# A new order for the last 900 of 1215 hand-ordered pieces of an attention and feed-forward kernel

## The chip, the cores and the metric

The kernel runs on one core of a Trainium2 chip. The time is device microseconds (us) of one execution; a kernel is run several times and its median is what counts. TensorE (PE in the profile) multiplies matrices and writes to the eight PSUM banks, P in the profile; ScalarE (ACT) and VectorE (DVE) read those banks, apply functions and write to on-chip memory; GpSimd (POOL) and SyncE (SP) mainly start DMA transfers. Each of these engines works through its own queue in order.

## The reference

Four batches, eight heads, 768 tokens, head size 64. Three of the heads (0, 2 and 6) use plain causal attention, the other five see only the first four tokens and a window of 64. The result, 3072 tokens by 512, goes through two matrix products with a leaky rectifier between them.

```python
scores = np.matmul(q, k.transpose(0, 1, 3, 2)) / np.sqrt(64)
keep = causal & (is_sink | in_window)      # heads 1, 3, 4, 5, 7
keep = causal                              # heads 0, 2, 6
a = softmax(np.where(keep, scores, -1e9))
x = np.matmul(a, v)                        # to 3072 x 512
h = x @ w_in                               # 512 x 2048
g = np.maximum(h, 0) + alpha * np.minimum(h, 0)
out = g @ w_out                            # 2048 x 512
```

## The kernel before, in words

**Units.** Heads are taken two at a time, four pairs for each batch, so there are 16 units of attention, numbered 0 to 15. A unit's first head has number 0 within it, the second number 1. The two heads of a unit lie in the upper and the lower 64 of the 128 partitions of the query tile `qT` and the key tile `kT`. Unit numbers that leave 0 when divided by four hold two causal heads, those that leave 2 one causal and one windowed head, the others two windowed heads.

**Pieces.** The work is cut into 1215 named pieces, and the list `ORDER` gives the order in which they are issued. Each engine's queue is this list with the other engines' work left out: there is no scheduler that moves anything. The names mean, for unit `n`, head `h` and part `m`:

- `Lq`, `Lk`, `Lv`: loads from memory, issued from SP; `C..`: casts of what was loaded; `Dq`, `Dk`: transposes by DMA, issued from SP, of the cast queries and keys; `T..`, `t..`: the same by TensorE for the early units.
- `Sn.h.m`: one part of the scores of a head, into one PSUM bank. `sn.h.m`: ScalarE's exponential of it (L512 for causal heads, L560 and L562 for windowed ones), which empties the bank. `mn.h.m`: VectorE's masking. `An.h`: probabilities times values (L595). `an.h`: VectorE's normalisation (L605, L606), which empties that bank. `Xn`: transpose into the token tile `xT`, by DMA for units 4 to 14.
- `Pt.f`: first feed-forward product for token block `t` (L640); `pt.f` and `gt.f`: rectifier on ScalarE (L645) and VectorE (L652). `O0.s.u` and `o0.s`: second product for block 0 (L660) and its copy out (L666). `Qt.u.y`, `Zt.u.y`, `Dy.h`, `b1` to `b8`: second product for blocks 1 to 7 in seven partial products (L718), with the sums before and after them.

**Banks.** A piece that needs a PSUM bank takes, when it is recorded, the one that was given back longest ago (`take`, `give`). In the chip it then waits for the engine that empties that bank.

**Score sets.** From unit 4 on, `S` pieces are not issued at their own place. They are gathered, and issued together at the first piece that may not pass them (`beside_burst`, `emit_burst`). A gathered set is issued in one of two ways. If both halves hold at least 576 columns, or the set has a unit from 8 on with two heads of one kind, L473 issues it with 64-row matmuls, alternating between the two heads, so that each head uses its own half of the array. Here this is called a *paired* set. Otherwise L466 issues it one matmul after the other on all 128 rows, the other head's rows being zero: an *unpaired* set.

```python
        halves = [[x for x in burst if x[1] == hh] for hh in range(2)]
        columns = [sum(x[5].shape[1] for x in half) for half in halves]
        if min(columns) < SPLIT and not any(merged(x[0]) for x in burst):
            for x in burst:
                nc.tensor.matmul(*x[3:6], start=True, stop=True)
        else:
            at = [0, 0]
            while halves[0] or halves[1]:
                hh = min((h for h in range(2) if halves[h]), key=lambda h: at[h])
                to, keys, queries = halves[hh].pop(0)[3:6]
                own = slice(D * hh, D * hh + D)
                nc.tensor.matmul(to, keys[own], queries[own], start=True, stop=True)
```

A part of a causal head has 448 columns (units 4, 8, 12) or 488 (units 6, 10, 14), a part of a windowed head 352 and the third one 448.

Of the kernel before, what the change touches and what calls it, by code (L numbers as in the profile page):

```python
# [26 lines left out]
g1.0 P0.5.1 Tk5 P0.4.0 p1.8 P0.6 tk5.0 g1.8 p0.7 P0.4.1 g1.12 P0.5.2 P0.4.2 p0.6 tk5.1 P0.10 g0.7 p0.4 p0.10 g0.6
S4.0.3 s4.0.3 S4.0.0 P1.4 g0.4 Tk6 g0.10 S4.0.1 S5.1.0 m4.0.3 P1.6 p0.5 tk6.1 Ck7.0 near1 D1.0 P0.12 tk6.0 O0.0.0 g0.5
O0.0.1 p1.6 Lv7 p0.12 g1.6 p1.4 S6.1.1 D1.1 s5.1.0 s4.0.0 S5.1.1 S4.1.2 g1.4 m4.1.0 s4.0.1 s4.1.2 Z1.0.1 s6.1.1 s5.1.1
O0.1.0 S5.0.0 S4.0.4 S4.1.4 S4.1.1 g0.12 O0.1.1 s5.0.0 m4.0.5 s4.1.4 m4.0.0 Ck7.1 s4.1.1 ns S5.1.2 S4.0.2 S4.1.3  # L30
S5.0.1 O0.0.2 s5.1.2 s4.1.3 D2.1 O0.0.3 O0.2.0 s5.0.1 m6.1.1 S6.0.4 s4.0.4 S5.0.2 S6.1.0 D4.1 m5.0.0 s4.0.2 Z1.0.3
S6.0.0 m5.1.2 o0.0 S6.1.2 S4.1.5 Lq9 Cq7 Cv4 s5.0.2 m5.1.1 O0.1.2 D2.0 Tk7 s4.1.5 O0.2.1 Cv5 Tq7 m4.0.1 m5.0.2 s6.1.0
m8.1.2 s6.1.2 O0.1.3 tk7.0 m5.1.0 m4.0.4 tk7.1 A4.0 Ck8 s6.0.0 tq7 A5.1 m4.1.2 S6.0.5 o0.1 m4.1.1 O0.2.2 Cq8 Dk8.0
s6.0.5 O0.3.0 S7.1.1 S6.0.1 a4.0 a5.1 S6.0.3 s6.0.4 S7.1.0 m6.1.0 m4.1.4 S7.0.2 S7.1.2 m5.0.1 s6.0.3 O0.2.3 m6.1.2 Ck9
A5.0 s7.1.2 O0.3.1 Cv6 m4.1.5 S6.0.2 Cv7 m4.1.3 s7.1.1 Dq8 s6.0.1 O0.3.2 m6.0.4 o0.2 a5.0 m6.0.5 S7.0.0 s7.1.0 Dk9.0
s7.0.2 A6.1 O0.3.3 m6.0.1 S7.0.1 Cq9 m7.1.0 s6.0.2 m6.0.0 s7.0.0 A4.1 m7.0.0 S8.0.0 S8.1.0 s7.0.1 S8.0.5 m6.0.3 S8.1.3
m7.1.1 S8.0.3 a6.1 S8.1.1 m7.1.2 o0.3 s8.0.3 A6.0 X5 a4.1 s8.0.5 A7.1 Q1.0.1 m7.0.2 s8.1.3 s8.1.0 m7.0.1 m6.0.2 s8.1.1
A7.0 a7.1 b1.1.0 Dq9 S9.1.1 a6.0 a7.0 S8.0.2 Lq10 S8.1.4 S8.0.1 X4 Q1.0.2 S9.1.0 S9.0.1 s8.0.0 Z1.0.2 D3.1 S9.0.2
# [958 lines left out]
```

## Time and profile before

| | |
|---|---|
| Times of three runs | 222.39, 222.77, 223.88 us; median 222.77 us |
| Profiled execution | span 220.4 us from first to last instruction; what lies around the span is not in the trace, and the median is 2.4 us above it |
| Granted TensorE clock | 1.000 over the whole span |
| Busy | PE 214.5 us (97%), DVE 188.0 (85%), ACT 145.8 (66%), POOL 45.6 (21%) |
| DMA | 35.98 MB, mean 163 GB/s |

A busy PE is one that has a matmul in flight; the end of a matmul is modelled, and matmuls overlap, so the mean duration of one is longer than the distance from one to the next. Where matmuls follow each other, the distance is what the next one costs. The chain in the profile follows the last instruction back to what released it, and so tells which engine sets the end.

### The profile page before, as it was taken

The numbers are of one execution on the slowest core, as the hardware profiler recorded it, in microseconds if no ns is written. First come the engines' busy times: TensorE is split into PE (matmuls) and PEld (weight loads), VectorE is DVE, ScalarE is ACT, GpSimd is POOL, SyncE is SP. The second block draws the span as 40 slices with busy tenths as digits, with TensorE's granted clock in tenths as the row PEclk, the third lists the DMA queues.
The fourth block names the chain that finished last, engine by engine and source line by source line (L and its number), as shares of the span: only waits on it lengthen the run. The fifth ranks groups of instructions, "written<-read, shape, count | busy, mean of one in ns | idle before, by whom it ended". The sixth has DMA issues, their size and how long they took to land.

```text
span 220.4 us, 5779 instructions
## 1 busy us (share of the span) xinstructions
PE 214.5 (97%) x2210; PEld 158.0 (72%) x2210; DVE 188.0 (85%) x471; ACT 145.8 (66%) x314; POOL 45.6 (21%) x92
## 2 busy tenths in 40 slices
PE   8989999999999999999999999999999999999993
PEld 7879866765465865577899666757889645888882
DVE  6879849979989897999998998999999767997841
ACT  4789659989999795657953165799783066816230
POOL 6679980620031200000004110100000200001000
PEclk9999999999999999999999999999999999999999
DMA  6999999999999999979999998791004310002124
GB/s 187 319 233 222 307 241 231 227 201 218 205 245 167 259 162 222 198 182 193 211 215 174 228 184 194 176 187 42 4 1 123 103 79 0 0 3 95 51 93 147
DMA packets 89655, 35.98 MB, mean 163 GB/s; under 512 B 76676, under 2 KB 87964, under 8 KB 89628
## 3 DMA queue, kind: packets, MB, share of 16 engines
q1 hardware_dynamic: 83484, 26.35, 59.4%
q0 software_dynamic: 5824, 8.93, 17.8%
q8 instruction: 17, 0.28, 0.5%
q10 hardware_dynamic: 320, 0.34, 0.5%
q14 instruction: 10, 0.08, 0.1%
HBM read 27.58 MB, written 6.29 MB: 154 GB/s over the span
## 4 chain that ended last, share of the span: by engine, by line
PE 92%; DVE 3%; ACT 2%; issue 1%
PE P L640 36%; PE P L718 28%; PE P L595 7%; PE P L660 7%; PE P L473 4%; PE P L814 3%; PE P L456 2%; PE P L406 2%; PE P L466 1%; PE P L620 1%; DVE kT L435 1%; PE P L544 1%; DVE g L652 1%; ACT neg L645 1%; ACT kT L435 0%
## 5 line engine op out<-in xcount | busy, mean ns | idle before, releaser
L640 PE MATMUL P<-xT,w_in_b 128*128 128x512 bf16 (+1 forms) x512 | 89.6, 326 | 0.0
L652 DVE SCALAR_TENSOR_TENSOR g<-neg,oma,P 128x256 bf16<-128x256 f32 (+1 forms) x128 | 71.7, 607 | 11.4 <-ACT neg L645 11.0
L645 ACT ACTIVATE neg<-P 128x512 f32<-128x512 f32 x96 | 55.4, 602 | 30.3 <-PE P L640 15.7
L640 PEld LDWEIGHTS <-w_in_b 128*128 128x128 bf16 x512 | 49.2, 98 | 29.1 <-issue 0.3
L718 PEld LDWEIGHTS <-g 128*128 128x128 bf16 x480 | 45.7, 98 | 8.1 <-issue 0.8
L512 ACT ACTIVATE eR<-P 128x448 bf16<-128x448 f32 (+4 forms) x63 | 37.0, 627 | 4.8 <-PE P L505 2.2
L718 PE MATMUL P<-w_out_b,g 128*128 128x256 bf16 x320 | 39.0, 273 | 0.0
L736 POOL DMA_DIRECT2D out_dram<-ot x14 | 7.6, 545 | 115.6 <-ACT ot L760 37.9
L560 ACT ACTIVATE eS<-P 128x352 bf16<-128x352 f32 x45 | 20.8, 494 | 2.3 <-PE P L473 1.4
L606 DVE TENSOR_TENSOR xn<-P,rcp 128x448 bf16<-128x448 f32 (+1 forms) x32 | 19.4, 607 | 1.1
L571 DVE TENSOR_TENSOR eS<-eS,ms_near 128x352 bf16<-128x352 bf16 x45 | 15.8, 363 | 0.7 <-ACT eS L560 0.6
L660 PE MATMUL P<-w_out_b,g 128*128 128x512 bf16 x64 | 15.8, 379 | 0.2 <-ACT kT L429 0.2
L703 DVE TENSOR_TENSOR g<-g 128x1024 bf16<-128x1024 bf16 x20 | 13.7, 683 | 0.1
L456 PE MATMUL P<-qT,kT 128*128 128x192 bf16 (+14 forms) x68 | 11.1, 251 | 0.2 <-ACT eS L566 0.2
L595 PEld LDWEIGHTS <-eS 128*128 128x128 bf16 x260 | 10.0, 97 | 1.3
L595 PE MATMUL P<-vb,eS 128*128 128x65 bf16 x260 | 10.8, 193 | 0.0
L522 DVE TENSOR_TENSOR eR<-eR,mr_near 128x128 bf16<-128x128 bf16 (+5 forms) x54 | 10.6, 223 | 0.0
L473 PE MATMUL P<-qT,kT 64*128 64x176 bf16 (+10 forms) x164 | 10.4, 249 | 0.0
L718 PE MATMUL P<-w,g 128*128 128x256 bf16 x80 | 10.4, 273 | 0.0
L660 PEld LDWEIGHTS <-g 128*128 128x128 bf16 x64 | 5.6, 97 | 6.3 <-issue 1.1
L595 PE MATMUL P<-vb,eR 128*128 128x65 bf16 x276 | 10.0, 193 | 0.0
L595 PEld LDWEIGHTS <-eR 128*128 128x128 bf16 x276 | 9.4, 97 | 0.6 <-issue 0.2
(130 smaller groups left out, 267.8 us busy)
## 6 DMA issues: line engine op xcount, KB each, us to landing
out_dram<-ot POOLq DMA_DIRECT2D x18, 256.0 KB, 3.2
rows<-in_k_dram SPq DMA_DIRECT2D x21, 192.0 KB
rows<-in_q_dram SPq DMA_DIRECT2D x18, 192.0 KB
rows<-in_v_dram SPq DMA_DIRECT2D x17, 192.0 KB
rows<-in_v_dram SPq DMA_DIRECT2D x14, 196.0 KB
rows<-in_q_dram SPq DMA_DIRECT2D x7, 384.0 KB
w_out_b<-in_moe_w_out_dram POOLq DMA_DIRECT2D x4, 512.0 KB, 15.1
rows<-in_k_dram SPq DMA_DIRECT2D x9, 196.0 KB
```

Of the source, the lines that this page charges most:

```text
L456: nc.tensor.matmul(to, keys, queries, start=True, stop=stop)
L473: nc.tensor.matmul(to, keys[own], queries[own], start=True, stop=True)
L512: nc.scalar.activation(ebuf[n, hh][:, lo:hi].rearrange("p (x c) -> p x c", x=len(parts)), P[:, got[0]:got[0] + len(parts), 0:(hi - lo) // ...
L560: nc.scalar.activation(slots, sc[:, 0:352].rearrange("p (s c) -> p s c", c=176), AF.Exp, scale=scale)
L571: nc.vector.tensor_tensor(slots, slots, ms_near[:, 0:2, :] if m == 0 else ms_near[:, 1:3, :], op=ALU.mult)
L595: nc.tensor.matmul(pav[:, i, :], e[:, o:o + 128], vv[:, j, hh, 0:D + 1], start=(m == 0), stop=(m == len(terms) - 1))
L606: nc.vector.tensor_tensor(xn[n][:, 0:nt, D * hh:D * hh + D], pav[:, :, 0:D], rcp.to_broadcast([128, nt, D]), op=ALU.mult)
L640: nc.tensor.matmul(psg[:, w * i:w * (i + 1)], w_in_b[:, c, 128 * fb:128 * (fb + 1)], xT[:, c, o:o + w], start=(x == 0), stop=(x == 3))
L645: nc.scalar.activation(neg[t, f], bank(held["P", t, f][0]), AF.Relu, scale=-1.0)
L652: nc.vector.scalar_tensor_tensor(g_buf[t % 2][:, fb, 0:w], neg[t, f][:, c], oma[:, fb:fb + 1], bank(got[0])[:, c], op0=ALU.mult, op1=ALU.add)
L660: nc.tensor.matmul(bank(held["O", t, s][0]), g_buf[t % 2][:, f, 128 * s:128 * (s + 1)], w_out_b[:, f, :], start=(f == 0), stop=(f == 15))
L718: nc.tensor.matmul(q_bank(t, u, CHAIN[y]), left[t, u][y][:, f, :], right[y][:, f, :], start=(first and f == 0), stop=(f == 7), skip_group_ ...
```

## The change

Only the list `ORDER` changes. It holds the same 1215 names. Of the first 303, three (`m4.0.2`, `m8.0.2` and `m12.1.2`) go to later places; these three issue no instruction, since no mask ends in that part, so the first 300 of the new list do what the first 303 of the old one did. All others come in another order. SP's queue, with its loads, transposes and stores, has the same 152 instructions in the same order, and so has GpSimd's. TensorE has 2210 matmuls before and after, VectorE 471 instructions, ScalarE 316 with its three DMA issues.

What the new list does to the score sets follows from the functions above. The columns are those of the first and the second head. The first five sets (4.0.5; 4.1.0; 4.0.3; 4.0.0; 4.0.1 with 5.1.0) are the same in both, and unpaired; they have 2592 columns in 11 matmuls.

| Before: pieces in a set | columns | | After: pieces in a set | columns | |
|---|---|---|---|---|---|
| 6.1.1 5.1.1 4.1.2 | 0, 1152 | unpaired | 4.1.5 | 0, 448 | unpaired |
| 5.0.0 4.0.4 4.1.4 4.1.1 | 800, 896 | paired | 6.1.2 | 0, 448 | unpaired |
| 5.1.2 4.0.2 4.1.3 5.0.1 | 800, 896 | paired | 5.1.1 4.0.4 4.1.1 5.0.2 6.1.0 5.0.1 | 1248, 1152 | paired |
| 6.0.4 5.0.2 6.1.0 6.0.0 6.1.2 4.1.5 | 1424, 1248 | paired | 4.0.2 6.1.1 5.0.0 5.1.2 | 800, 800 | paired |
| 6.0.5 | 488, 0 | unpaired | 4.1.3 6.0.5 6.0.0 4.1.4 6.0.3 4.1.2 | 1464, 1344 | paired |
| 7.1.1 6.0.1 6.0.3 7.1.0 7.0.2 7.1.2 | 1424, 1152 | paired | 6.0.4 | 488, 0 | unpaired |
| 6.0.2 | 488, 0 | unpaired | 6.0.1 7.1.1 7.0.1 7.0.2 7.1.0 7.1.2 | 1288, 1152 | paired |
| 7.0.0 | 352, 0 | unpaired | 7.0.0 | 352, 0 | unpaired |
| 7.0.1 | 352, 0 | unpaired | 6.0.2 | 488, 0 | unpaired |
| 8.0.0 8.1.0 8.0.5 8.1.3 8.0.3 8.1.1 | 1344, 1344 | paired | 8.0.3 8.1.1 8.0.4 8.0.0 8.0.5 8.1.4 | 1792, 896 | paired |
| 9.1.1 8.0.2 8.1.4 8.0.1 | 896, 800 | paired | 9.1.1 9.0.2 9.1.2 9.0.1 9.0.0 8.1.5 | 1152, 1248 | paired |
| 9.1.0 9.0.1 9.0.2 8.1.2 | 800, 800 | paired | 8.0.2 9.1.0 8.0.1 8.1.3 | 896, 800 | paired |
| 8.1.5 8.0.4 9.0.0 9.1.2 | 800, 896 | paired | 10.1.1 8.1.0 10.0.1 10.0.3 | 976, 800 | paired |
| 10.1.0 | 0, 352 | unpaired | 11.1.1 10.1.0 10.1.2 10.0.2 10.0.5 11.0.1 8.1.2 10.0.4 | 1816, 1600 | paired |
| 10.0.1 10.0.4 | 976, 0 | unpaired | 10.0.0 | 488, 0 | unpaired |
| 10.0.0 | 488, 0 | unpaired | 11.0.0 11.1.0 11.0.2 11.1.2 | 800, 800 | paired |
| 10.0.3 | 488, 0 | unpaired | 13.0.2 12.0.0 12.1.5 12.1.0 | 896, 896 | paired |
| 10.0.5 10.1.2 11.0.1 11.1.1 10.1.1 11.0.2 | 1288, 1152 | paired | 13.0.0 12.0.3 12.1.4 13.1.0 | 800, 800 | paired |
| 10.0.2 11.0.0 11.1.2 11.1.0 | 840, 800 | paired | 12.1.3 12.0.4 12.0.5 13.1.2 | 896, 896 | paired |
| 12.0.0 12.1.2 | 448, 448 | paired | 12.1.1 12.0.1 12.1.2 12.0.2 | 896, 896 | paired |
| 12.1.4 12.0.2 12.0.5 13.1.0 | 896, 800 | paired | 14.1.2 13.0.1 14.0.5 13.1.1 | 840, 800 | paired |
| 12.0.1 13.1.2 12.1.5 13.0.0 | 800, 896 | paired | 14.0.2 | 488, 0 | unpaired |
| 12.1.0 12.1.3 13.0.1 12.0.3 | 800, 896 | paired | 14.0.4 | 488, 0 | unpaired |
| 12.0.4 12.1.1 14.1.2 13.1.1 14.0.3 13.0.2 | 1384, 1248 | paired | 14.1.1 14.0.3 14.0.1 15.1.1 14.0.0 15.1.2 | 1464, 1152 | paired |
| 14.0.2 | 488, 0 | unpaired | 14.1.0 15.0.1 15.0.0 15.1.0 15.0.2 | 1152, 704 | paired |
| 14.0.4 | 488, 0 | unpaired | | | |
| 14.0.1 | 488, 0 | unpaired | | | |
| 15.1.2 14.1.1 14.0.5 15.0.0 14.0.0 15.1.1 | 1328, 1152 | paired | | | |
| 15.0.2 15.1.0 15.0.1 14.1.0 | 800, 704 | paired | | | |

The diff, cut to the stretches that the prediction speaks of:

```diff
 ORDER = """
 ...
-S4.0.3 s4.0.3 S4.0.0 P1.4 g0.4 Tk6 g0.10 S4.0.1 S5.1.0 m4.0.3 P1.6 p0.5 tk6.1 Ck7.0 near1 D1.0 P0.12 tk6.0 O0.0.0 g0.5
-O0.0.1 p1.6 Lv7 p0.12 g1.6 p1.4 S6.1.1 D1.1 s5.1.0 s4.0.0 S5.1.1 S4.1.2 g1.4 m4.1.0 s4.0.1 s4.1.2 Z1.0.1 s6.1.1 s5.1.1
 ...
-b8.3.0 g4.14 P5.8 s12.0.0 S12.1.4 p5.12 s12.1.2 S12.0.2 b6.3.0 S12.0.5 S13.1.0 Lk15 P5.6 Dq14 s12.0.5 p5.8 g5.12 p5.6
 ...
+S4.0.3 s4.0.3 S4.0.0 P1.4 g0.4 Tk6 g0.10 S4.0.1 S5.1.0 m4.0.3 P1.6 p0.5 tk6.1 Ck7.0 near1 D1.0 P0.12 tk6.0 O0.0.0 p1.6
 ...
+Cq9 s6.0.1 s7.0.1 O0.3.2 S7.0.0 A4.1 s7.1.0 s7.0.2 m6.0.5 m7.0.2 s7.0.0 a4.1 S6.0.2 s7.1.2 Q1.0.1 S8.0.3 s6.0.2 s7.1.1
+m7.1.0 m6.0.4 m6.0.0 m6.0.3 S8.1.1 S8.0.4 S8.0.0 S8.0.5 m7.1.1 S8.1.4 b1.1.0 m6.0.1 X5 s8.0.4 s8.0.0 Z1.0.2 O0.3.3
+m7.1.2 Dq9 m7.0.1 o0.3 s8.0.5 m7.0.0 kfz2 A6.0 A7.1 Lq10 A7.0 a6.0 Q1.0.2 s8.1.1 a7.1 s8.1.4 S9.1.1 S9.0.2 s8.0.3 S9.1.2
+a7.0 S9.0.1 S9.0.0 S8.1.5 X4 s9.1.1 X6 s9.1.2 Q1.0.6 s9.0.2 D3.0 X7 Q1.0.5 s9.0.0 b2.1.0 S8.0.2 S9.1.0 m8.0.4 s9.0.1
 ...
+s8.1.2 m10.0.1 Z2.0.3 m10.1.1 s10.0.2 s11.1.1 s11.0.1 Lk12 Q2.1.5 s10.0.5 b4.2.1 Cv10 P3.2 s10.0.4 Cv11 Z2.0.2 Q2.1.6
 ...
+b6.3.0 Cq14 P4.0.0 g5.12 P4.0.1 p5.8 p4.7 g4.7 P5.10 s13.0.2 s12.1.0 g5.8 s12.1.5 S13.0.0 p4.0 S12.0.3 p5.10 m12.1.5
+S12.1.4 g4.0 S13.1.0 s13.0.0 m13.0.2 g5.10 s12.0.3 P5.4 m8.1.2 Q4.0.1 p5.4 s12.0.0 Q4.1.1 Dq14 Z4.0.1 s13.1.0 b1.4.0
+s12.1.4 S12.1.3 S12.0.4 S12.0.5 S13.1.2 s13.1.2 Q4.0.2 Dk14.1 g5.4 P5.14 m4.1.2 b1.4.1 Z4.0.3 s12.0.4 s12.1.3 S12.1.1
 ...
```

120 lines of the change are left out of this document (57 added, 63 removed).

## The prediction, made before the changed kernel had run

> **What bounds the kernel now.** I read the page's first lines, then the busy times by stretch, then TensorE's waits, then the chain.
>
> ```profile
> span 220.4 us, 5779 instructions
> ...
> PE 214.5 (97%) x2210; PEld 158.0 (72%) x2210; DVE 188.0 (85%) x471; ACT 145.8 (66%) x314; POOL 45.6 (21%) x92
> ...
> PE 92%; DVE 3%; ACT 2%; issue 1%
> ```
>
> The third line is the chain by engine: TensorE sets the end for 92% of the span. By stretches (columns: stretch, its length, busy us of PE, its weight loads, DVE, ACT, POOL, then granted clock, DMA share, GB/s):
>
> ```profile
> 20.00:55.00 35.00, 34.80 (x354) 24.14 (x352) 27.79 (x67) 29.52 (x57) 16.75 (x35) 1.00 1.19 237
> 55.00:114.00 59.00, 59.00 (x622) 39.66 (x622) 55.89 (x153) 45.77 (x113) 6.17 (x10) 1.00 1.10 206
> 114.00:140.00 26.00, 26.00 (x241) 18.85 (x239) 24.16 (x54) 11.47 (x24) 3.71 (x7) 1.00 0.97 193
> 140.00:165.00 25.00, 25.00 (x272) 19.01 (x271) 24.69 (x70) 22.07 (x54) 1.63 (x3) 1.00 0.40 75
> 165.00:218.00 53.00, 51.75 (x477) 40.15 (x475) 40.15 (x88) 22.34 (x52) 2.68 (x5) 1.00 0.21 69
> ```
>
> From 55 us on, where the new order begins to differ (O0.0.0 stands just before it), PE is never idle up to its last matmul; in the last stretch the 1.25 us missing are the end. A busy PE could still be a slow one, so two more views: all that PE waited for between 20 and 218 us, and two long pieces of the chain (start, length, what).
>
> ```profile
> PE P L660 <- ACT kT L429: 0.2, 1, 0.2
> ```
>
> ```profile
> 173.79 12.95 PE P L640 x60
> 200.93 15.84 PE P L718 x144
> ```
>
> One wait of 0.2 us, in the part that stays. 60 matmuls of 512 columns in 12.95 us are 0.216 us each, 144 of 256 columns in 15.84 us 0.110 each: (0.216 - 0.110) / 256 = 0.414 ns a column and 4 ns a matmul, the same rate in both places. So the time behind 55 us is PE's work, laid end to end. A new order can change it in two ways only: by the work in the score sets, and by waits where there are none now.
>
> **The change: score sets.** All other matmuls stay as they are. The price of a paired set comes from a large and a small one, of 1344 columns a head and of 448; each is followed by another line's matmul, so the distance of the starts is its cost.
>
> ```profile
> 73.12 0.75 PE L473 MATMUL P<-qT,kT 64*128 64x448 bf16 x11
> 73.80 0.38 PE L595 MATMUL P<-vb,eR 128*128 128x65 bf16 x7
> ```
>
> ```profile
> 140.12 0.36 PE L473 MATMUL P<-qT,kT 64*128 64x448 bf16 x2
> 140.42 0.50 PE L718 MATMUL P<-w,g 128*128 128x256 bf16 x3
> ```
>
> 0.68 and 0.30 us: (0.68 - 0.30) / (1344 - 448) = 0.424 ns for a column of the longer head, and 0.11 us fixed. The 2688 columns of the large set cost 0.25 ns each, against 0.414 one after the other: the two heads do run side by side, and the longer one sets the time.
>
> Now the table of sets is added up. Unpaired columns: before 9192 in 40 matmuls, after 6280 in 30. Paired, by the longer head of each set: before 17,352, after 19,272. Paired sets: 17 before and 17 after, so the fixed cost stays. In all 26,544 columns become 25,552: 992 fewer. At 0.414 ns that is 0.41 us, and ten unpaired matmuls at 4 ns are 0.04. **The sum of the work: -0.45 us.** It is small because the new sets are fuller but not better balanced: the shorter heads leave 1704 columns empty before and 2632 after (the set from 8.0.3 alone 1792 against 896).
>
> The Trainium skill, page "TensorE: Matmul & The Clock Gate", section "Back-to-back issue gap", gives for streams of loads and matmuls a sustained 81 ns at 128 columns and 131 ns at 512. By that slope, 0.13 ns a column, the 992 columns would be an estimated 0.13 us; the trace has 0.216 us for 512 columns, so the trace's rate stands.
>
> **The change: waits.** Here nothing can be gained, since PE waits for nothing now; only lost. What is new is how many banks a set takes at once: at most six before, once eight after. I looked where PE, if it ran without a stop, would reach work whose bank is still to be emptied. The rows: unpaired parts and other PE work from the chain, durations of groups, and ScalarE's pace in a run without idle time.
>
> ```profile
> 69.91 0.21 PE P L466 x2
> 70.12 0.87 PE P L660 x4
> 70.99 0.15 PE P L466 x2
> ...
> 72.55 0.64 PE P L595 x21
> ...
> 75.18 0.87 PE P L718 x8
> ```
>
> ```profile
> L640 PE MATMUL P<-xT,w_in_b 128*128 128x512 bf16 x256 | 60.0, 379 | 0.0
> ...
> L560 ACT ACTIVATE eS<-P 128x352 bf16<-128x352 f32 x45 | 20.8, 494 | 2.3 <-PE P L473 1.4 <-PE P L466 0.9
> ...
> L606 DVE TENSOR_TENSOR xn<-P,rcp 128x448 bf16<-128x448 f32 x24 | 15.0, 624 | 0.8
> ...
> L605 DVE RECIPROCAL rcp<-P 128x7 f32<-128x7 f32 x24 | 4.8, 198 | 1.8 <-PE P L595 1.7
> ```
>
> ```profile
> 68.00 0.46 ACT L560 ACTIVATE eS<-P 128x352 bf16<-128x352 f32 x1
> 68.34 0.26 ACT L562 ACTIVATE eS<-P 128x96 bf16<-128x96 f32 x1
> 68.47 0.48 ACT L560 ACTIVATE eS<-P 128x352 bf16<-128x352 f32 x1
> 68.82 0.61 ACT L512 ACTIVATE eR<-P 128x488 bf16<-128x488 f32 x1
> 69.27 0.63 ACT L666 COPY ot<-P 128x512 f32<-128x512 f32 x1
> ```
>
> ScalarE's starts lie 0.35 us apart behind a part of 352 columns, 0.13 behind 96, 0.45 behind 488. A matmul's result is there 0.16 us after the next one begins (379 ns against 216).
>
> *Place one, the set from 8.0.3.* ScalarE must first finish the set from 6.0.1: s6.0.1, six windowed parts with two short ends, s6.0.2, the last being s7.1.1, whose bank the new set needs. From that older set's first matmul: 0.2 + 0.16 until 6.0.1's scores are there, then 2 x 0.45 + 6 x 0.35 + 2 x 0.13 = 3.26, and 0.11 for the last one's tail: 3.7 us. PE by then has done the set (0.11 + 1288 x 0.424 = 0.66), 7.0.0 and 6.0.2 (0.15, 0.21), O0.3.2 (0.87), A4.1 (0.64) and Q1.0.1 (0.87): 3.40, and gets 0.2 further before it comes to that bank. It waits about 0.1 us; nothing at all if ScalarE runs a little closer than these rows, 0.6 if it comes late to s6.0.1, behind the copy o0.2 (0.47 from row to row behind 69.27).
>
> *Place two, Q1.0.6.* It takes a7.0's bank. VectorE does a6.0, a7.1 and a7.0 in a row, 3 x (0.198 + 0.624) = 2.47, plus 0.16; PE meanwhile A7.1 and A7.0 (13 matmuls each at 0.64 / 21: 0.79), Q1.0.2 (0.87) and the set from 9.1.1 (0.11 + 1248 x 0.424 = 0.64): 2.30. A wait of 0 to 0.4.
>
> *Place three, the eight-bank set.* Q2.1.5 right behind it needs the bank of s10.1.0, whose scores are second in their half: 704 x 0.424 + 0.16 + 0.494 = 0.95 us, against 0.11 + 1816 x 0.424 = 0.88 for the set. A wait of 0 to 0.2.
>
> Their ends together are 0 and 1.2 us. A start that PE finds late makes the next wait shorter, since the emptying engine has gained on it, so I take **+0.2 us**. No wait is charged elsewhere: VectorE and ScalarE do the same work, and the tail behind Q6.1.4 is issued in nearly the old order.
>
> Sum: -0.45 + 0.2 = -0.25 us, against the span 220.4, so 220.15; what lies around the span, 2.4 us to the median of 222.77, stays. **222.5 us.**
>
> **The rivals.**
>
> *Banks emptied too late.* Fuller sets hand ScalarE more parts at once, and places of the three kinds come again in the sets from 12.1.1 and 14.1.1. For it: the sums at the three places, which come out within a few tenths of zero. Against more than a few tenths at each: ScalarE is busy for 45.77 of 59 us and 22.07 of 25, so it can be late in bursts, but not on the whole. Price: all three ends, 1.2 us, less 0.45: 223.5. It decides from 0.45 us of waits on: beyond that the change is **slower than before**. The Trainium skill, "TensorEngine Tiling (Array Packing)", section "PSUM Bottleneck", states this rule: tiling speeds up TensorE but not the emptying of PSUM. Before, the trace does not show it: PE waits for none of its 17 paired sets.
>
> *VectorE becomes the bound.* It has 24.69 of 25 us at 140 to 165 and 55.89 of 59 before. For it: each idle stretch that the new order opens there cannot be made good, as 0.31 us are all that is left. Against it: total work is the same, and Cv14 leaves the full stretch for an earlier one. Two to four us lost would give 224.3 to 226.3.
>
> *The transposes come late.* SP issues in order; Dq14 now waits for Cq14, which has moved behind the first P4.0 piece, and Dk14.1, Dk14.0 and Dq15 queue behind it.
>
> ```profile
> 140.45 1.22 SPq L358 DMA_TRANSPOSE qT<-natq  x1
> 141.72 3.16 SPq L381 DMA_TRANSPOSE kT<-natk  x2
> 144.98 1.84 SPq L358 DMA_TRANSPOSE qT<-natq  x1
> ```
>
> ```profile
> 151.88 0.76 PE L473 MATMUL P<-qT,kT 64*128 64x128 bf16 x13
> ```
>
> Dq14 and the two Dk14 are issued in 4.4 us, and the first set that needs them came 11.4 us after Dq14 began. Now PE has between Cq14's place and the set from 14.1.2: P4.0 (0.86), P5.10, P5.4, P5.14 and six Q4 products (nine at 0.87) and three sets (0.11 + 0.424 x 800 or 896, 1.43): 10.1 us. Room shrinks by 1.3 us of 7; it costs nothing unless landing takes over 5 us, and a microsecond if it does: 223.3.
>
> *It does not do what it says.* Were paired heads not side by side, 2912 more paired columns would bring nothing: 222.8. The large set's 0.25 ns a column speaks against it.
>
> **How the numbers follow.** The forecast, work saved and up to 0.45 us of waits, 222.3 to 222.8: 0.55. Banks too late, 222.8 to 224: 0.26. VectorE: 0.08; transposes: 0.05; no effect: 0.04; a gain that no row here explains: 0.02. The range takes in the forecast, the banks and the spread of the median (three runs lie 222.39 to 223.88): 221.8 to 223.8. Within 1%, 2.2 us, is about what a measurement can tell from no change. Faster by that needs five times the work that is saved: 0.02. Slower by that needs 2.7 us of waits, VectorE's case in the main: 0.08. The same: 0.90.
>
> **What would show it.** In the changed kernel's profile: L473 with 174 matmuls and L466 with 30; PE's waits, if any, for ACT L512 or L560 just ahead of L473, or for DVE L606 ahead of L718; the chain still over 90% PE; the set from 8.0.3 at about 0.87 us. I am wrong if PE shows idle time of over 1 us behind 55 us, or if its rate outside the sets is no longer 0.216 us for 512 columns.

## The result, and the profile after

The changed kernel takes 224.09 us (median of 8 runs, 223.81 to 225.22), the kernel before 222.91 us (8 runs, 222.39 to 223.88): a ratio of 1.0053 with a 95% interval of 1.0034 to 1.0073. It is 1.2 us slower. The forecast was 222.5 us, a gain of 0.25, and the range ended at 223.8. The profiled execution took 224.34 us, its span 222.63; the 1.71 us around the span are what the old order has too (223.32 less 221.61 in its second profile). One of the twelve executions of the run "new, Lq10 earlier" below was in a slower state, 227.03 us against 222.39 to 224.46 for the others, and the ratio of that run leaves it out.

First the page of the changed kernel: its span, the busy times, and the chain by engine.

```profile
span 222.6 us, 5788 instructions
...
PE 215.3 (97%) x2210; PEld 157.8 (71%) x2210; DVE 186.9 (84%) x471; ACT 146.4 (66%) x314; POOL 46.1 (21%) x92
...
PE 74%; DMA 7%; ACT 5%; DVE 5%; POOL 3%; issue 3%; SPq 1%; ACTq 0%; DVEq 0%; POOLq 0%
```

PE has 992 columns less to do and is busy 0.8 us longer. That alone says that the new time is hidden in rows that count as busy. The chain has 74% of PE where the prediction said over 90. This share moves with the execution: in later profiles of the unedited new order it is 84, 86 and 81%, in the second profile of the old order 90%.

The busy times by stretch (columns as in the prediction: stretch, length, PE, its weight loads, DVE, ACT, POOL, clock, DMA share, GB/s):

```profile
20.00:55.00 35.00, 34.44 (x360) 24.29 (x358) 27.75 (x66) 28.93 (x54) 17.12 (x36) 1.00 1.17 235
55.00:114.00 59.00, 58.57 (x610) 38.43 (x608) 54.72 (x149) 45.63 (x109) 6.17 (x10) 1.00 1.01 195
114.00:140.00 26.00, 26.00 (x252) 19.24 (x250) 24.75 (x61) 12.64 (x31) 4.11 (x7) 1.00 1.13 212
140.00:165.00 25.00, 24.97 (x253) 18.18 (x251) 23.89 (x65) 21.11 (x51) 1.62 (x3) 1.00 0.40 94
```

VectorE has not become the bound: it is less full than before in the second and fourth stretch. PE shows 0.46 us of idle time behind 55 us. All that PE waited for between 55 and 221 us, by the view of waits (engine, line, for whom: us, times, longest):

```profile
PE P L717 <- DVE xn L605: 0.3, 1, 0.3
```

One wait of 0.3 us is not 1.2. The rest is found with the prediction's own price of a set, 0.11 us and 0.424 ns for each column of the longer head, held against the starts of PE's rows (start, length, line, shapes, number of matmuls; a wait that is seen as idle time stands in brackets):

```profile
74.50 1.19 PE L472 MATMUL P<-qT,kT 64*128 64x64 bf16 x12
75.62 1.04 PE L659 MATMUL P<-w_out_b,g 128*128 128x512 bf16 x4
...
79.06 0.71 PE L472 MATMUL P<-qT,kT 64*128 64x176 bf16 x15
80.04 1.03 PE L717 MATMUL P<-g 128*128 128x256 bf16 x8 [0.26 <-DVE xn L605]
...
81.88 0.55 PE L472 MATMUL P<-qT,kT 64*128 64x448 bf16 x7
82.36 1.36 PE L639 MATMUL P<-xT,w_in_b 128*128 128x512 bf16 x5
```

```profile
107.16 0.97 PE L472 MATMUL P<-qT,kT 64*128 64x448 bf16 x17
108.23 1.03 PE L717 MATMUL P<-g,own 128*128 128x256 bf16 x8
```

```profile
163.10 1.00 PE L472 MATMUL P<-qT,kT 64*128 64x488 bf16 x11
164.03 1.05 PE L717 MATMUL P<-w_out_b,g 128*128 128x256 bf16 x8
```

From the start of a set to the start of what follows it:

| Set from | columns | price | from start to start | over the price |
|---|---|---|---|---|
| 8.0.3 (place one) | 1792 | 0.87 | 1.12 | 0.25 |
| 9.1.1, then Q1.0.6 (place two) | 1248 | 0.64 | 0.98 | 0.34 |
| 8.0.2 | 896 | 0.49 | 0.48 | 0 |
| 11.1.1, then Q2.1.5 (place three) | 1816 | 0.88 | 1.07 | 0.19 |
| 14.1.1 | 1464 | 0.73 | 0.93 | 0.20 |

The set from 8.0.2 and the twelve other sets that meet nothing late hold the price to 0.01 us; four places are late by 0.98 us together. In each of the four the waiting matmul starts 0.05 us behind the end of the instruction that empties its bank: 74.94 us behind 74.89 (ScalarE's s7.1.1, L559), 80.04 behind 79.99 (VectorE's a7.0, L605), 108.23 behind 108.17 (ScalarE's s10.1.0, L559), 163.63 behind 163.57 (ScalarE's copy b6.4.0, L759). Only one of them ends in a row with idle time before it. In the others the matmul that waits stands inside a group of matmuls, and its wait counts as that group's length: the row of the set from 8.0.3 is 1.19 us long and has 0.25 us of waiting in it.

Start times summed over the whole part from O0.0.0 to the last matmul confirm the work: before 164.525 us, after 164.954 (164.846 in the second profile). Other matmuls cost 1.24 us less (ten unpaired ones and their columns), paired sets 0.80 more, -0.44 in all. The waits are +0.99, and 0.11 more at P2.15.0. Three small waits of the old order, 0.17 together, went. That makes +0.49, against +0.43 measured.

The groups of the score matmuls are as the prediction said (before 164 and 40):

```profile
L472 PE MATMUL P<-qT,kT 64*128 64x176 bf16 (+10 forms) x174 | 11.6, 251 | 0.1
...
L465 PE MATMUL P<-qT,kT 128*128 128x176 bf16 (+11 forms) x30 | 4.6, 253 | 0.0
```

Two more differences lie outside that part. From the start of the last matmul to the end of the span it is 3.92 us before (3.78 in the second profile) and 4.09 after. And the start of O0.0.0, which the change should not touch, came at 51.95 before and at 53.59 after; that one varies with each execution (below).

So the profiles explain about 0.6 us: 0.33 to 0.43 in the part behind O0.0.0, 0.2 to 0.3 at the end. The times say 1.2, and 1.5 in the first repetition. The experiments had to find the rest.

### The profile page after: what moved, and what is told of

The parts are those of the page before. It is cut to its first block, busy times and chain, and to the rows that moved or that the text cites. A ratio compares the mean times of both kernels' runs of the same rounds, so it can differ in the third digit from the quotient of the medians.

```text
span 222.6 us, 5788 instructions
## 1 busy us (share of the span) xinstructions
PE 215.3 (97%) x2210; PEld 157.8 (71%) x2210; DVE 186.9 (84%) x471; ACT 146.4 (66%) x314; POOL 46.1 (21%) x92
## 4 chain that ended last, share of the span: by engine, by line
PE 74%; DMA 7%; ACT 5%; DVE 5%; POOL 3%; issue 3%; SPq 1%; ACTq 0%; DVEq 0%; POOLq 0%
PE P L639 31%; PE P L717 27%; PE P L659 6%; PE P L594 5%; DMA rows<-in_q_dram 5%; PE P L472 4%; DMA rows<-in_k_dram 3%; DVE g L651 2%; ACT neg L644 2%; POOL w_in_b L818 1%; ACT eS L559 1%; POOL vb L390 1%; DVE kT L434 1%; PE P L405 1%; POOL g L363 1%
## 5 line engine op out<-in xcount | busy, mean ns | idle before, releaser
L651 DVE SCALAR_TENSOR_TENSOR g<-neg,oma,P 128x512 bf16<-128x512 f32 (+1 forms) x128 | 71.6, 608 | 9.7 <-ACT neg L644 9.1
L644 ACT ACTIVATE neg<-P 128x512 f32<-128x512 f32 x96 | 54.4, 600 | 28.4 <-PE P L639 20.6
L511 ACT ACTIVATE eR<-P 128x448 bf16<-128x448 f32 (+4 forms) x63 | 36.4, 623 | 5.5 <-PE P L504 2.8
L717 PE MATMUL P<-w_out_b,g 128*128 128x256 bf16 x320 | 39.9, 273 | 0.0
L559 ACT ACTIVATE eS<-P 128x352 bf16<-128x352 f32 x45 | 20.1, 481 | 2.7 <-PE P L472 2.5
L605 DVE TENSOR_TENSOR xn<-P,rcp 128x448 bf16<-128x448 f32 (+1 forms) x32 | 19.4, 608 | 1.1
L570 DVE TENSOR_TENSOR eS<-eS,ms_near 128x352 bf16<-128x352 bf16 x45 | 14.5, 334 | 0.0
L472 PE MATMUL P<-qT,kT 64*128 64x176 bf16 (+10 forms) x174 | 11.6, 251 | 0.1
L455 PE MATMUL P<-qT,kT 128*128 128x192 bf16 (+14 forms) x68 | 11.1, 251 | 0.2 <-ACT eS L565 0.2
L472 PEld LDWEIGHTS <-kT 64*128 64x128 bf16 x174 | 6.8, 94 | 5.0 <-issue 4.6
L594 PE MATMUL P<-vb,eR 128*128 128x65 bf16 x276 | 10.1, 192 | 0.0
```

What stands on the lines that cost most here:

```text
L511: nc.scalar.activation(ebuf[n, hh][:, lo:hi].rearrange("p (x c) -> p x c", x=len(parts)), P[:, got[0]:got[0] + len(parts), 0:(hi - lo) // ...
L559: nc.scalar.activation(slots, sc[:, 0:352].rearrange("p (s c) -> p s c", c=176), AF.Exp, scale=scale)
L570: nc.vector.tensor_tensor(slots, slots, ms_near[:, 0:2, :] if m == 0 else ms_near[:, 1:3, :], op=ALU.mult)
L594: nc.tensor.matmul(pav[:, i, :], e[:, o:o + 128], vv[:, j, hh, 0:D + 1], start=(m == 0), stop=(m == len(terms) - 1))
L605: nc.vector.tensor_tensor(xn[n][:, 0:nt, D * hh:D * hh + D], pav[:, :, 0:D], rcp.to_broadcast([128, nt, D]), op=ALU.mult)
L644: nc.scalar.activation(neg[t, f], bank(held["P", t, f][0]), AF.Relu, scale=-1.0)
```

## The experiments

All times below, each against runs of the kernel before on the same chip. The first four runs of the table shared one chip, the next four a second, the other eight a third. "Part" is the time from O0.0.0 to the start of the last matmul, "end" the time from there to the end of the span, both from the profiled execution.

| Run | us, median (runs) | ratio to before, 95% interval | part | end |
|---|---|---|---|---|
| old order again | 223.00 (12) | 0.9997, 0.9970 to 1.0024 | 164.52 | 3.78 |
| new order again | 224.58 (12) | 1.0064, 1.0035 to 1.0092 | 164.85 | 4.08 |
| longer head first | 224.25 (12) | 1.0054, 1.0021 to 1.0088 | 165.74 | 4.09 |
| three heads not normalised | 223.68 (10) | 1.0042, 1.0011 to 1.0073 | 165.35 | 4.07 |
| old, other half of xT | 222.50 (12) | 1.0008, 0.9988 to 1.0028 | 164.52 | 3.73 |
| new, other half of xT | 222.83 (12) | 1.0023, 1.0005 to 1.0041 | 164.84 | 4.08 |
| old, quick emptying | 221.84 (12) | 0.9979, 0.9956 to 1.0002 | 164.45 | 3.75 |
| new, quick emptying | 222.12 (12) | 0.9988, 0.9973 to 1.0003 | 164.13 | 4.06 |
| new order, third | 223.99 (12) | 1.0038, 1.0007 to 1.0070 | 165.52 | 4.07 |
| new, Lq10 earlier | 223.28 (12) | 1.0003, 0.9973 to 1.0033 | 164.84 | 3.75 |
| new, four drains on SP | 223.47 (12) | 1.0028, 1.0001 to 1.0055 | 164.84 | 4.06 |
| new, all mends | 224.45 (12) | 1.0045, 1.0016 to 1.0073 | 165.43 | 3.71 |
| new, Lq10 behind X7 | 223.93 (12) | 1.0031, 1.0012 to 1.0050 | 165.46 | 4.07 |
| old, load ahead of X6 | 224.13 (12) | 1.0035, 1.0010 to 1.0059 | 165.89 | 3.79 |
| new order, fourth | 223.95 (12) | 1.0030, 1.0010 to 1.0050 | 164.84 | 4.08 |
| new, mended | 223.31 (12) | 1.0005, 0.9985 to 1.0024 | 165.27 | 3.92 |

The new order unedited was thus timed four times: 1.0053, 1.0064, 1.0038, 1.0030. It is slower than before in each, by 0.7 to 1.5 us, 1.0 in the mean.

### The two orders again

No edit; the files as they are.

> The old order, unchanged, once more: what one profile and one median are worth. Theory 'banks' (the new order costs time at a handful of places where a bank is emptied too late, 0.26 + 0.34 + 0.19 + 0.20 us in its profile, against 0.44 us of work saved): ratio 1.000 within 0.003; from O0.0.0 to the last matmul 164.5 us again; the time up to O0.0.0, 51.95 us in the first profile, may come out up to 1.6 us later, as it did in the profile of the new order. Rival 'start' (the new order's loss lies ahead of O0.0.0 and behind the last matmul): O0.0.0 again at 52.0 within 0.3 us.

> The new order, unchanged, once more. 'Banks': ratio 1.003 to 1.007; from O0.0.0 to the last matmul 165.0 us again, with the same four waits; O0.0.0 anywhere between 52 and 53.6 us. 'Start': ratio 1.005 again and O0.0.0 again at 53.6, 1.0 us or more behind that of the old order's profile in the same job.

The loss is there again, 1.0064. The second profile of the new order has the same four waits to 0.001 us (from start to start 1.121, 0.976, 1.063 and 0.931 us, against 1.122, 0.976, 1.063 and 0.932) and the same end; P2.15.0 has none this time. The waits for banks are therefore fixed by the order. The start of O0.0.0, 53.32 in the old order and 53.04 in the new, shows that its 1.6 us of difference in the first pair belonged to those executions.

### Place one: the longer head first

```diff
+                rest = [sum(x[5].shape[1] for x in half) for half in halves]
                 hh = min((h for h in range(2) if halves[h]), key=lambda h: at[h])
+                if max(columns) - min(columns) > 300:
+                    hh = 0 if rest[0] >= rest[1] else 1
```

> The new order with one thing changed: in a set whose heads differ by more than 300 columns (those from 8.0.3, 14.1.1 and 14.1.0) the longer head is issued first until the rest is even, so that the shorter head's banks are asked for later. Work is the same. 'Banks': the wait of 0.26 us in the set from 8.0.3 (it asks for s7.1.1's bank 0.15 us after its start, now 0.37 us later at the least) goes, and of the 0.20 us in the set from 14.1.1 some 0.13; from O0.0.0 to the last matmul 164.6 us, 0.35 to 0.4 less than with the new order alone. Rival: the sets are dear because they are unbalanced, not because of the bank: unchanged, 165.0.

Place one's wait is gone, and the one at the set from 14.1.1 fell from 0.20 to 0.08; places two and three stayed. The part did not get shorter but 0.9 us longer, by a single new wait at P2.15.0 (view of waits, line numbers moved by three):

```profile
PE P L642 <- ACT eS L562: 1.2, 1, 1.2
```

The ScalarE instruction named had ended long before. What P2.15.0 also needs is xT, which the DMA transposes X4, X5 and X6 write; X4 landed at 82.89 us, and P2.15.0 began at 82.94. Behind O0.0.0, PE came there 0.25 us earlier and went on 1.0 us later than in the unedited order.

### Place two: three heads not normalised

```diff
+        if (n, hh) in ((6, 0), (7, 0), (7, 1)):
+            nc.vector.tensor_copy(xn[n][:, 0:nt, D * hh:D * hh + D], pav[:, :, 0:D])
+            give(got)
+            return
```

> The new order, with a6.0, a7.1 and a7.0 left without the division by their sums (a copy instead of reciprocal and product: three reciprocals of 0.2 us less on VectorE). 'Banks': a7.0 ends 0.4 to 0.6 us earlier and Q1.0.6's wait of 0.34 us goes; the other three waits stay; from O0.0.0 to the last matmul 164.6 us. Rival: Q1.0.6 waits for something else that ends at the same time (an exponential or a transpose): less than 0.1 us gained.

This kernel leaves out the division of three heads by their sums. Place two's wait went, so it was VectorE's three evictions in a row, as the prediction said. And again P2.15.0 waited (X4 landed at 81.70 us, P2.15.0 began at 81.74):

```profile
PE P L643 <- ACT eR L511: 0.7, 1, 0.7
```

Two different cures of bank waits, one result: PE gets to the transposes earlier and stands there. That made theory T: transposes that come late in many executions are the part of the loss that the first two profiles don't show. Theory W said that bank waits and the end are all.

### No wait for transposes

```diff
-        o = o // S % 2 * SX + o % S
+        o = (o // S + (t == 2)) % 2 * SX + o % S
```

> Old order; the P2 products read batch 0's half of xT, which has long been there, so they wait for no DMA transpose (the numbers that they give are of the wrong batch; the work is the same). In the profile of before no matmul waited at that place. Every theory expects the time of before, 222.7 to 223.3 us. If transposes that come late now and then cost the old order too, its highest times (up to 225.5) come down and the median falls by up to 0.3.

> The same edit in the new order. Theory T, that P2.15.0 finds its transposes late in many executions (0.11 us in one profile, none in another, 0.74 and 1.27 where PE came there earlier) and that this is the part of the loss which the profiles don't show: 0.4 to 0.8 us less than the new order's 224.1 to 224.6, so 223.3 to 223.8, a ratio of 1.002 to 1.003. Theory W, that the four waits for banks and the end are all of it: only the 0 to 0.1 us that the profiles show goes, 224.0 to 224.5, ratio 1.005.

The old order gains nothing (1.0008). The new order's loss against it shrinks to 0.33 us, where it was 0.8 to 1.6 in the pairs with transposes. Its part is 164.84, with the four bank waits in it. That agrees with T: with that dependence gone, what is left is within the 0.3 in the part and 0.3 at the end that the profiles show. It does not prove T by the time, since the unedited new order was not timed on this chip, and the interval of 1.0023 overlaps those of the unedited order on the other two.

### No wait for banks either

```diff
+        if n >= LAY:
+            hi = lo + 64
         nc.scalar.activation(ebuf[n, hh][:, lo:hi]...
-            nc.scalar.activation(slots, sc[:, 0:352]...
+            nc.scalar.activation(slots[:, :, 0:32], sc[:, 0:352]...[:, :, 0:32], ...
```

These two kernels also have the edit to the half of xT and the three heads without the division.

> Old order, with the edit of the transposes and with quick emptying: from the fourth pair of heads on ScalarE takes exp of 64 columns of each part instead of 448 to 488, and of 2 x 32 instead of 2 x 176 (the rest of the exponentials are left out, the masks and products work on old contents), and three heads are copied without the reciprocal. PE's work is untouched and it had no waits behind 55 us: 222.5 to 223.2 us, part behind O0.0.0 164.4 to 164.5 us.

> The same three edits in the new order: banks are emptied at once, so the waits of places one, two, three and of the set from 14.1.1 must go. Theory W (waits 1.0 us, end 0.25, work -0.45): the part behind O0.0.0 comes out 0.4 to 0.5 shorter than in g1, the end 0.25 longer, and the time 0.1 to 0.3 us below g1. If something else in the new order costs time in executions that the profiles did not catch: 0.3 to 0.8 us above g1. If a paired column is not the work that I counted, the part behind O0.0.0 isn't shorter than in g1.

The part is 0.32 us shorter in the new order than in the old one. One wait of 0.20 survived, at the set from 14.1.1: it isn't for an exponential but for the copy b6.4.0, which empties Q4.0.4's bank and stayed as it was. Without it, and without 0.10 us that g1 still waits at Q6.0.4, the work makes -0.42, the prediction's -0.45. The end is 0.31 longer. Sum zero; the medians differ by 0.28, the new order being the slower one, where 0.1 to 0.3 us less had been expected, and the intervals overlap. So even with all of these banks but one emptied at once the new order gains nothing that could be measured here.

### The transposes seen: the third profile of the new order

> The changed kernel unedited, as the base on the chip of these runs: 224.1 to 224.6 us, ratio 1.005 to 1.006. Part behind O0.0.0 164.85 to 164.95 us when its transposes are in time in the profiled execution, up to 165.7 when not; end 4.06 to 4.09 us.

This execution shows the late transpose in the unedited kernel (rows of PE around P2.15.0, then the view of waits):

```profile
81.53 0.55 PE L472 MATMUL P<-qT,kT 64*128 64x448 bf16 x7
82.68 0.60 PE L639 MATMUL P<-xT,w_in_b 128*128 128x512 bf16 x2 [0.59 <-ACT eR L511]
```

```profile
PE P L639 <- ACT eR L511: 0.6, 1, 0.6
```

The set from 8.0.2 takes 0.48 us elsewhere; here the next start is 1.15 behind it, 0.67 late. The records of the landings tell which transfer it was: X4's last part landed at 82.63, P2.15.0 began at 82.68. The whole picture, in us, from the issues on SP, the landings, and the starts of the matmuls that need them (the first of that piece for X4, the third for X6):

| Run | X4 issued, landed | needed at | X6 issued, landed | needed at |
|---|---|---|---|---|
| before | 74.57, 79.84 | 80.64 | 76.95, 80.51 | 81.08 |
| old order again | 75.93, 81.22 | 82.00 | 78.31, 81.89 | 82.44 |
| after | 76.89, 81.99 | 82.36 | 78.47, 82.87 | 82.92 (late) |
| new order again | 76.38, 81.32 | 81.82 | 77.93, 82.23 | 82.27 |
| new order, third | 76.69, 82.63 | 82.68 (late) | 78.13, 83.10 | 83.14 |
| new order, fourth | 75.22, 80.31 | 81.28 | 77.39, 81.42 | 81.72 |
| longer head first | 76.49, 82.89 | 82.94 (late) | 77.82, 83.31 | 83.38 |
| new, Lq10 earlier | 74.85, 77.65 | 81.62 | 77.73, 80.66 | 82.06 |

In the old order X4 lands 0.8 us and X6 0.6 us ahead of need. In the first two profiles of the new order it is 0.4 to 0.5 us for X4 and nothing for X6, in the third nothing for either, in the fourth 1.0 and 0.3. The room is smaller because PE comes to the first P2 piece as soon after O0.0.0 as before (28.78 us against 28.68), while X4 is issued later, 22.7 to 23.5 us behind O0.0.0 (before 22.6), and X6, whose issue begins at the same distance, takes longer to issue in three of the four. SP's rows (start, length, line, two transposes X6 and X7), before and after:

```profile
76.95 2.87 SPq L614 DMA_TRANSPOSE xT<-xn  x2
```

```profile
78.47 3.72 SPq L613 DMA_TRANSPOSE xT<-xn  x2
```

X7 takes 1.24 in both; X6 takes 1.54 before and 2.38 after (1.25 to 2.38 in the four profiles of the new order). With so little room, what varies from execution to execution goes into the time: P2.15.0's wait was 0.11, 0.01, 0.67 and 0 us in the four, 0.2 in the mean.

The Trainium skill, page "Perfetto Trace Analysis", section "DMA Instruction — HWDGE (DVE, Sync)", says that the recorded span of such an issue covers the lock and the making of the descriptors, and that the movement of the data isn't in it. This case agrees: in the runs of the table X4's issue took 1.2 to 1.4 us, its landing came 2.8 to 6.4 us behind the start of the issue.

### The load ahead of them: Lq10

Just ahead of X4 on SP goes Lq10, two loads of 192 KB. It stands there in the old order too, and there too X4 lands 5.3 us behind its issue; what the new order took away is the room. If the load goes elsewhere, the room should come back.

```diff
-... kfz2 A6.0 A7.1 Lq10 A7.0 a6.0 ...
+... kfz2 A6.0 A7.1 A7.0 a6.0 ...
-... S6.0.4 s4.1.2 Dk8.0 s6.0.3 ...
+... S6.0.4 s4.1.2 Lq10 Dk8.0 s6.0.3 ...
```

> New order, with the load Lq10 (two transfers of 192 KB) moved up to where SP is idle before Dk8.0, so that it isn't on its way just ahead of X4, X6 and X7. Theory T (late transposes are the part that the profiles of the new order don't show): the loss shrinks by most of what the edit to the other half of xT took away, to 223.2 to 223.7 us, ratio 1.001 to 1.003. If the load has nothing to do with it: ratio 1.005 to 1.006 as without the edit. The four waits for banks stay as they are.

X4 landed 2.80 us after its issue instead of 4.9 to 5.9, and X6 was issued in 1.21 (SP's row for X6 and X7):

```profile
77.73 2.75 SPq L613 DMA_TRANSPOSE xT<-xn  x2
```

The ratio came out at 1.0003 beside 1.0038 of the unedited kernel; the intervals overlap, so the time doesn't show the gain, only the landings do. The end also fell, to 3.75 (next experiment but one).

The other way round, in the old order:

```diff
-... S8.1.2 X6 s8.1.4 ...
+... S8.1.2 Lq11 X6 s8.1.4 ...
-m9.0.0 Lq11 P2.7.0 ...
+m9.0.0 P2.7.0 ...
```

> Old order, with the load Lq11 (two transfers of 192 KB) moved up to just ahead of X6. Theory T: X6's issue ends later than the 26.54 us behind O0.0.0 of before, by 0.5 us or more, the first P2 product waits as in the new order, and the time rises by 0.3 to 1 us, ratio 1.002 to 1.005. If a transpose's landing doesn't hang on the loads ahead of it: 0.999 to 1.001.

A load ahead of X6 is enough to make the old order as slow as the new one, 1.0035. X6's issue took 2.46 us, and the wait, here put down to the right cause, stands at the third matmul of the first P2 piece, the one that reads X6's rows:

```profile
78.81 3.79 SPq L614 DMA_TRANSPOSE xT<-xn  x2
```

```profile
81.89 0.61 PE L640 MATMUL P<-xT,w_in_b 128*128 128x512 bf16 x2
83.70 1.02 PE L640 MATMUL P<-xT,w_in_b 128*128 128x512 bf16 x4 [1.21 <-DMA xT<-xn]
```

From start to start it is 1.38 us over the usual 0.22, and the part is longer by 1.37.

The second cure in the new order puts the load behind X7 and its cast Cq10 on with it:

```diff
-... A7.1 Lq10 A7.0 ... X7 Q1.0.5 ... m9.1.0 Cq10 P2.6.0 ... P2.1.1 m9.0.0 ...
+... A7.1 A7.0 ... X7 Lq10 Q1.0.5 ... m9.1.0 P2.6.0 ... P2.1.1 Cq10 m9.0.0 ...
```

> New order, with Lq10 moved behind X7 and its cast Cq10 moved on accordingly, so that no load is issued ahead of X4 and X6. Theory T: X6's issue on SP takes 1.2 to 1.5 us instead of 2.1 to 2.4, P2.15.0 doesn't wait in the profile (28.78 us behind O0.0.0), and the time falls below i3's by 0.4 to 0.9 us, ratio to before 1.001 to 1.003. If the load has no part in it: X6's issue and the ratio stay as in i3.

> The changed kernel unedited, as the base on this chip: ratio 1.004 to 1.006; X6's issue 2.0 to 2.4 us; P2.15.0 28.78 us behind O0.0.0 if its transposes are in time, up to 29.4 if not; end 4.07.

The transposes did what T said: X6 issued in 1.39, landed 1.0 us ahead of need; X4 took 4.6 us to land and was in time too. The time did not fall: 1.0031 beside 1.0030. The set from 10.1.1 is late by 0.46 us and P3.4 by 0.15, waits that only the two kernels with the moved cast have; part of the first is seen as idle time, and its releaser is VectorE:

```profile
104.00 0.52 PE L472 MATMUL P<-qT,kT 64*128 64x280 bf16 x5
104.69 0.36 PE L472 MATMUL P<-qT,kT 64*128 64x488 bf16 x1 [0.18 <-DVE g L651]
104.99 1.92 PE L717 MATMUL P<-w_out_b,g 128*128 128x256 bf16 x16
```

This looks like the prediction's rival of VectorE on a small scale: a cast taken out of a place where it cost nothing, and paid for 15 to 20 us later. No run moves the cast alone, so the cast is the likely cause and not a shown one. And the base shows how much of T is luck: the fourth profile of the new order had X6 issued in 1.25 us, where 2.0 to 2.4 had been expected, and no late transpose at all.

### The end

```diff
+    item("p99", lambda: [nc.sync.drain() for _ in range(4)])
-... s4.1.2 Dk8.0 s6.0.3 ...
+... s4.1.2 p99 Dk8.0 s6.0.3 ...
```

> New order, with four more instructions in SP's stream that do nothing (drains, before Dk8.0, where SP is idle). In all new-order profiles one of SP's closing waits comes 0.39 us after the one before it, in all old-order profiles 0.06 to 0.08, although the transfers had landed. If that is a fixed place in SP's stream that comes into the open when the stream is a few instructions shorter, the end falls from 4.07 to 4.09 us to about 3.75 and the time by 0.3 us (223.8 to 224.3). If it hangs on the stores themselves, the end stays 4.07 to 4.09.

SP closes the program with a row of waits for transfers and engines. The start times of two neighbours among them, behind the landing of the last store, in us:

```
before            219.181  219.246
old order again   220.400  220.464
after             221.045  221.434
new order again   220.393  220.783
new, third        221.250  221.640
Lq10 earlier      220.187  220.266
four drains       220.283  220.348
```

0.39 in each profile of the unedited new order, 0.06 to 0.08 in each of the old. Four instructions that do nothing, 150 us earlier, took the gap from this place, and so did "Lq10 earlier", which adds one wait to SP's stream; "Lq10 behind X7", which adds none, kept the 0.39. The trace has 217 instructions of SP in every profile with the gap, 218 or 219 in the old order (whose transfers are the same, but which needs one or two waits more), 218 with Lq10 earlier, 221 with the drains. So it is a place in SP's stream and not the stores. The drains did not remove the gap but moved it: with them, here and in the last version below, SP's first closing wait began 0.65 us behind the start of the last matmul, 0.34 to 0.35 in all profiles without drains, though what it waits for had come 37 us before. There it costs nothing, since SP then waits for landings anyway. ("All mends", with the drains and one wait more, doesn't show where it went.) What SP does in the gap no view shows. In the run with the drains the last store itself landed later, 2.82 us behind the start of the last matmul against 2.48 to 2.49 in the unedited new order, so its end stayed at 4.06 and the ratio, 1.0028, proves nothing; in "all mends", with the same drains, the end is 3.71. The size of this term is 0.3 us by the gaps.

### Mended versions

All cures at once: Lq10 and the drains ahead of Dk8.0, the longer head first, and

```diff
-... Z4.1.2 S14.0.3 s14.0.5 ... m13.0.1 b6.4.0 S15.1.2 ...
+... Z4.1.2 S14.0.3 b6.4.0 s14.0.5 ... m13.0.1 S15.1.2 ...
```

> New order with Lq10 earlier, the four drains, the longer half of an uneven set issued so that both halves end together, and b6.4.0 ahead of s14.0.5. Expected gone: the wait at place one (0.26), at the set from 14.1.1 (0.20), late transposes, 0.32 us of the end; left: places two and three (0.34 and 0.19). Part behind O0.0.0 about 164.35 us (before: 164.52), end about 3.75, time 222.4 to 223.0 us, ratio 0.998 to 1.000. If an earlier arrival of PE only finds the next bank later, the part stays at 164.8 and the ratio at 1.002.

A miss: 1.0045. Earlier is not better for b6.4.0: the copy now holds up s14.0.5 on ScalarE, which ends at 164.27 us, and the set from 14.1.1, whose next matmul begins at 164.32, waits 0.56 us instead of 0.20. And moving Lq10 ahead of Dk8.0 and Dq8 put those two in X4's position: Dq8's last part landed at 74.96, and the set from 8.0.3, which needs it, began at 75.09 (the view names a ScalarE instruction). In the run "new, Lq10 earlier", with the same move, Dq8 landed 0.8 us ahead of that set, so the move alone need not bring this wait:

```profile
75.09 0.92 PE L475 MATMUL P<-qT,kT 64*128 64x64 bf16 x12 [0.43 <-ACT eS L562]
```

The last version keeps b6.4.0, has the longer head first, Lq10 behind X7, and the drains:

> New order with Lq10 behind X7, the longer half of uneven sets first, and four drains on SP before Dk8.0. Expected: place one's wait (0.26) gone, the one at the set from 14.1.1 0.1 instead of 0.2, places two and three as they are (0.34, 0.19), no wait for transposes; part behind O0.0.0 164.4 to 164.6 us, SP's closing gap 0.06; time as before, ratio 0.998 to 1.002. So I don't expect it to beat the kernel before by more than can be measured.

1.0005, the kernel before once more. Place one is gone, 0.08 is left at the set from 14.1.1, no transpose is late, SP's gap is 0.06; but the two waits that came with the moved cast are there again, 0.46 at the set from 10.1.1 and 0.33 at P3.4, so the part is 165.27 us where 164.4 to 164.6 had been expected. No version here beats the kernel before, and the numbers say why: the order has 0.44 us to give, and places two and three alone take 0.53.

## Why the prediction was wrong, by its steps

**The work: right.** -0.45 us was predicted, -0.44 is measured in the first profile and -0.42 from the pair with quick emptying. 174 and 30 matmuls, 17 paired sets at 0.11 us and 0.424 ns a column: all as said, and the set price holds to 0.03 us where nothing waits (the largest miss is the set from 11.1.1 with quick emptying, 0.90 us for 0.88).

**The waits: the step that failed, by its size.** The prediction named three places with their releasers, added up their ends to 0 and 1.2 us, and took +0.2. All three came, for exactly these releasers: 0.25 at place one (0.1 said, 0.6 at most), 0.34 at place two (at most 0.4), 0.19 at place three (at most 0.2). A fourth, the set from 14.1.1, had only been mentioned among the rivals without a price, while the sum said that no wait is charged elsewhere: 0.20, for a bank that ScalarE's copy b6.4.0 empties. Together 0.98 where the sum has 0.2; less the 0.17 of small waits that the old order had and the prediction took for none, 0.8. The reason given for the low value was that a start PE finds late makes the next wait shorter. It does not: the places are 5, 28 and 56 us apart, and between them the emptying engines have long caught up. The waits add, and each is the same to 0.002 us in the four profiles of the unedited order. The middle of each place's range, or the sum at its upper end, would have been nearer than 0.2. The prediction's own sign of being wrong, over 1 us of idle time behind 55 us, did not come (0.46): it could not, since most of these waits count as busy time.

**The transposes: the mechanism was among the rivals, at another place.** I looked at Dq14 and Dk14, which SP issues 11 us ahead of need, and priced them at 5 in 100. X4 and X6, issued 4 to 6 us ahead of need, were not among them. Their room shrank from 0.8 and 0.6 us to 0.4 and 0.0 in the first profile. That costs nothing in one execution and 0.7 in another. How much on the average is only bounded: four profiles show 0.2 in the mean; by the times the loss is 0.7 to 1.5 us with it and, on another chip, 0.3 without, each known to about 0.5.

**What lies around stays, and the tail is in nearly the old order: wrong by 0.3 us.** From the start of the last matmul to the end of the last store's issue both orders take 1.08 us; what is longer is SP's closing gap, by 0.32.

**The rivals.** "Banks emptied too late" is what happened: the three places took 0.78 of the 1.2 us that gave its 223.5, and with the fourth place they make the order slower, as that rival said. The page of the Trainium skill that was named there, "TensorEngine Tiling (Array Packing)", section "PSUM Bottleneck", now has its row: the fuller set from 8.0.3 is 0.25 us over its price, for a bank. VectorE did not become the bound in the new order; in the two kernels that moved its cast, waits for it took 0.6 and 0.8 us. "It does not do what it says" is refuted by the work.

**The chances.** The time lies within 1% of before, where 90 in 100 were given; the range missed it by 0.3 us at its upper end, of which 0.14 is that the kernel before came out at 222.91 over eight runs and not at the 222.77 of three. The bounds of the waits were in it, the end and X4 were not.

**What stays open.** The waits, the work and the end make 0.6 us, late transposes 0.2 in the mean of four profiles; the times say 1.0 in the mean of four. The difference of 0.2 is within the intervals and is not explained. Why SP has 0.39 us between two closing waits. And the start of O0.0.0: 51.2 to 53.3 us in five profiles of old-order kernels (mean 52.4), 51.6 to 53.7 in thirteen of new-order ones (mean 52.9). The instructions up to there are the same, the two ranges cover each other, and 0.5 us between the means is no more than such spreads allow; it can't be excluded that some of the loss lies there.

## What to carry to other kernels

Where an engine shows no idle time, look for waits as the distance of starts above a price that you have from undisturbed rows, since a wait inside a group counts as busy; and add up the bounds of such waits place by place rather than let them cancel. An order that is full to the last microsecond has its slack in transfers: list, for each transfer that the path needs, issue, landing and need, and see what a reordering leaves of that room and which loads it puts ahead. When the work saved is 0.2% of the time, three waits of a quarter of a microsecond decide the sign.

## What the runs showed of the hardware that I had not expected

A transposing transfer lands later when the same engine issues loads just ahead of it: X4 landed 2.8 to 4.6 us after its issue in the four runs without the two loads of 192 KB just ahead, and 4.9 to 6.4 in the fourteen with them. The issue of X6 alone took 1.21 to 1.59 us in those four, 1.25 to 2.38 in the new order's others, and 2.46 with two loads directly ahead of it, so the load is not all that sets it.

A gap of 0.3 to 0.4 us in SP's closing waits moves with the number of instructions in SP's stream: four empty instructions 150 us earlier put it from the fifth closing wait to the first, where it costs nothing.
